# Three blocks of queries turned by VectorE, from 128-byte rows loaded through ScalarE's queue

## The chip, the cores and the metric

The kernel runs on one core of a Trainium2 chip. The metric is the device time in microseconds (us) of one execution. Executions of a kernel differ by some tenths of a per cent: the three of the kernel before took 1526.53, 1528.02 and 1528.81 us.

## What is computed

A linear attention, an RMS norm, and two feed-forward layers, all in float32 (batch 8, heads 8, sequence 576, head width 64; 4608 tokens of width 512; hidden width 2048):

```python
kv  = einsum('bhsd,bhse->bhde', k, v)
out = einsum('bhsd,bhde->bhse', q, kv)
x   = out / sqrt(mean(out * out, -1) + 1e-6) * g_norm     # heads side by side: 4608 x 512
h   = x @ w_in;   x = (max(h, 0) + alpha * min(h, 0)) @ w_out
h   = x @ w_in2;  x = (h / (1 + exp(-1.702 * h))) @ w_out2
```

## The kernel before

**Tiling.** The 4608 tokens are nine blocks of 512 (j = 0 to 8). Each float32 matrix is split into a high and a low part that TensorE multiplies as float32r, so a product is three matmuls of 128x512 (`mm3`, L1078). Blocks 1 to 8 go through the layers in pairs with a scheme that needs seven products instead of eight (`pair_in`, `pair_out`); block 0, half of the hidden width of block 1, and of block 2, go through plainly (`plain`, `gemm_in`, `gemm_out`).

**Stages.** First comes block 0's attention. Then `plain` walks the list `segs` of the first layer: block 0's hidden chunks 0 to MH-1, block 1's chunks 0 to 7, block 0's chunks MH to 15, block 2's chunks 0 to 7, two sets of six or twelve matmuls per chunk and direction. After that `pairs` runs the pairs of both layers. The weights are converted as the kernel runs (`weight`, `sums`: ScalarE, VectorE, GpSimd) and written to DRAM, from where SyncE's queue (SP) loads them back piece by piece (L1266).

**Attention of the later blocks.** For block j, `job_q_later` has SP load the queries of its 512 tokens, all heads, in 256-byte rows (one row is one head of one token; L639), 128 tokens in each of four DMAs, one more where a block lies across two batches. For each pair of heads p, TensorE turns the four 128x128 pieces into one PSUM bank (L655), and ScalarE copies the bank to the tile `qT` (L663). `job_out` multiplies `qT` with the batch's key-value product (L684), ScalarE copies the result out (L729), and the norm follows. `job_x` has VectorE turn the normed block in squares of 32x32 (L755). These jobs are dealt among the steps of the main line by the table JOBS (block: first half step, number of half steps); J1 does so for block 1. So blocks 6 to 8 fall into the first half of `pairs`.

**Order.** Every operation is first noted (`note`) with its engine and a cost. A planner in the kernel (`arrange`) then lays all of them out in time, with due times made of the constants (AHEAD, SPARE, SHIFT, the ..._WAY triples, RINGS and others) and a list OPENING for the first microseconds, and gives out buffers; each engine then executes its instructions in the order so found. That order is fixed when the kernel is built: on the chip, an engine whose next instruction waits doesn't take a later one.

**A bank's turn in `pairs`.** Steps with two hidden chunks alternate, and each step is six matmuls in, six out. A first-layer bank (X, Z) is written by six matmuls, copied out by ScalarE (L1362) or added by VectorE (L1354), and written again after three other groups of six.

Of the kernel before, what the change touches and what calls it, by code (L numbers as in the profile page):

```python
# [10 lines left out]
F32 = mybir.dt.float32  # L11
# [8 lines left out]
P = 128  # L20
# [1 line left out]

LAG = 2

MH = 6
EARLY = ()


# [1 line left out]
SEQ = "q0 q1 o0 q2 q3 x0 x1 o1 x2 x3"  # L30

K1 = (0, 1)
J1 = (1, 6)


PLAIN = 3
HALF = 4
KEPT = 4
MID = 0
SUM_SLACK = -20.0  # L40
XD = 2

JOBS = {2: (12, 12), 3: (32, 12), 4: (43, 12), 5: (63, 23), 6: (100, 16), 7: (124, 22), 8: (153, 16)}


P_IN = (1, 2, 6, 5, 3, 7, 4)
# [7 lines left out]

MM, TR, ACT, DVE, POOL, ISSUE, LAND, RATE, HOP = 0.227, 0.109, 0.63, 0.67, 1.27, 0.55, 2.2, 0.335, 0.2
ACT2, DVE2, POOL2 = 1.06, 1.17, 2.8
KB1, B128, B256, B512 = 1.1, 2.9, 1.77, 1.3

HOP_ASIDE = 0.8
AHEAD = {'wt': 9.6, 'xs': 30.3, 'xc': 40.9, 'gr': 7.1, 'ld': 13.7, 'raw': 50.7, 'w2p': 46.7, 'x': 14.7}  # L60
SLACK = 10.0
SPARE = {'8': 1, '4': 3, '2': 2}
SPARE_W = {'8': 1, '4': 2, '2': 7}

BACKLOG = 2.0
URGENT = 10.0
LD_LOW = {'4': 15}
ADDS = 4
PASSES = 1
AHEAD_START = {'wt': 22.5, 'xs': 24.0, 'xc': 74.6, 'gr': 8.0, 'ld': 16.2, 'raw': 299.2, 'w2p': 67.1, 'x': 12.0}  # L70
AHEAD_LATER = {'wt': 5.4, 'xs': 64.6, 'xc': 171.8, 'gr': 8.1, 'ld': 7.1, 'raw': 192.8, 'w2p': 20.7, 'x': 11.7}
SPARE_LATER = {'8': 3, '4': 6, '2': 6}
SPARE_W_LATER = {'8': 4, '4': 1, '2': 1}
LD_LOW_LATER = {'4': 15}
EARLY_T = 420.0
LEAD = 25.0
START_T = 60.0
AFTER = {}
OPENING = {
# [14 lines left out]
}  # L94
FILLED = 42.0
WAKE, SPARE_TIME = 2.5, 0.7
LATE = 0
START_WAY = (0.74, 28.59, 3.37)
FIRST_WAY = (1.12, 18.86, 1.66)
LATER_WAY = (1.14, 8.81, 1.95)  # L100
SHIFT = {
# [20 lines left out]
}  # L122
SEED = 14
GAP, SLOW = 1.8, 3.4

RINGS = (3, 1, 2, 9)

UNITS = 110
UNIT = 512
# [8 lines left out]
def linear_attention_two_ffn_kernel(  # L138
# [120 lines left out]
    def spare_of(now, later):  # L259
        return now if pe_clock[0] < EARLY_T else later  # L260
# [20 lines left out]
    def tl(key):  # L281
        return tiles[key]

    def arrange(before, first, later, shift, stop=None):
# [6 lines left out]
        for o in ops:  # L291

            if o.eng == "PE":
                o.early = o.clock < EARLY_T
                o.late = before[o.n] if before and not o.early else o.clock + LEAD
                now_ = o.late + o.cost
                o.base = o.late
            else:
                o.late = now_ + o.slack if o.slack is not None else 1e9
                o.early = now_ < EARLY_T + LEAD  # L300
            o.land = o.cost + (LAND + o.mb / RATE if o.eng == "SP" else 0.0)
        for o in reversed(ops):
            o.way = START_WAY if o.early and o.clock < START_T else first if o.early else later
            late = [a.late - o.way[2] * (HOP if a.eng != o.eng else 0.0) - o.land for a in after[o.n]]
# [127 lines left out]
        for _ in range(len(ops)):  # L432
# [33 lines left out]
            start[o.n] = t  # L466
            free_at[o.eng] = t + cost
            fin[o.n] = t + cost
            if o.eng == "SP":
                dma_at = max(dma_at, t + cost) + o.mb / RATE  # L470
                fin[o.n] = dma_at + LAND
            changed = {o.eng}
# [54 lines left out]
    def runs(t0, n):  # L527
        done = 0
        while done < n:
            b, s = divmod(t0 + done, S)  # L530
            step = min(n - done, S - s)
            yield done, step, b, s
            done += step
# [66 lines left out]
    def job_q(j, p):  # L600

        if j:
            return job_q_later(j, p)
        bank, qT, src = ("qTps", j, p), ("qT", j, p), ("ldq", j, p)

        def load():
            for h in range(2):
                nc.sync.dma_start(
                    out=tl(src)[:, h * TB // 2 : (h + 1) * TB // 2],
                    in_=q[0, 2 * p + h, 0:TB, :].rearrange("(p t) d -> p (t d)", t=NT4),  # L610
                )

        def fn():
            for t in range(NT4):
                to = tl(bank)[:, t * P : (t + 1) * P]
                nc.tensor.transpose(to[0:D], tl(src)[:, t * D : (t + 1) * D], ident)
                nc.tensor.matmul(to[D:P], lhsT=tl(src)[:, (NT4 + t) * D : (NT4 + t + 1) * D], rhs=ident, start=True, stop=True)

        note(
            "SP", 2 * ISSUE, load, writes=[(src, 0)], new=[(src, [P, TB], F32, "2")],  # L620
            ahead=ahead_of("ld"), slack=None, mb=0.26 * KB1,
        )
        held_by[qT] = turn_of("qT", RINGS[3])
        note(
            "PE", 12 * TR, fn, reads=[(src, 0)], writes=[(bank, 0), held_by[qT]],
            new=[(bank, [P, TB], F32, "a")], aside=True, idle=lambda: tl(bank)[:, 0:P],
        )
        note(
            "ACT", ACT, lambda: nc.scalar.copy(tl(qT), tl(bank)), reads=[(bank, 0)], writes=[(qT, 0)],
            new=[(qT, [P, TB], F32, "2")], low={"2": 3},  # L630
        )

    def job_q_later(j, p):
# [30 lines left out]
            new=[(qT, [P, TB], F32, "2")], low={"2": 3},  # L664
        )

    def q_of(j, p):

        return ("qT", j, p), lambda: tl(("qT", j, p))

    def job_out(j, pp):

# [920 lines left out]
```

## Time and profile before

| | |
|---|---|
| median of three executions | 1528.02 us |
| profiled execution: its time, its span | 1526.27 us, 1524.5 us |
| TensorE busy | 1508.5 us (99%) |
| VectorE busy | 1165.7 us (76%) |
| ScalarE busy | 784.8 us (51%) |
| GpSimd busy | 338.3 us (22%) |
| queue of SP: share of the 16 DMA engines' span | 81.2% |

The span goes from the first to the last instruction; the time has 1.8 us more around it. An engine's busy time doesn't hold its waits, nor the instructions that issue a DMA, so an engine can be shown idle while it issues. Matmuls overlap (each is shown for some 390 ns and the next begins sooner), so what a matmul costs is read from start to start.

### The profile page before, as it was taken

The numbers are of one execution on the slowest core, as the hardware profiler recorded it, in microseconds if no ns is written. First come the engines' busy times: TensorE is split into PE (matmuls) and PEld (weight loads), VectorE is DVE, ScalarE is ACT, GpSimd is POOL, SyncE is SP. The second block draws the span as 40 slices with busy tenths as digits, with TensorE's granted clock in tenths as the row PEclk, the third lists the DMA queues.
The fourth block names the chain that finished last, engine by engine and source line by source line (L and its number), as shares of the span: only waits on it lengthen the run. The fifth ranks groups of instructions, "written<-read, shape, count | busy, mean of one in ns | idle before, by whom it ended". The sixth has DMA issues, their size and how long they took to land.

```text
span 1524.5 us, 19956 instructions
## 1 busy us (share of the span) xinstructions
PE 1508.5 (99%) x7430; PEld 1244.7 (82%) x7430; DVE 1165.7 (76%) x1175; ACT 784.8 (51%) x985; POOL 338.3 (22%) x298
## 2 busy tenths in 40 slices
PE   8999999999999999999999999999999999999999
PEld 6787878788888888888888888888888888888887
DVE  5999997988789999998999776556665665557511
ACT  5875764545554655545556555445544554445222
POOL 3487727402100335133416210000000000000000
PEclk9999999999999999999999999999999999999999
DMA  9996898989987899979999976687668666766970
GB/s 285 298 324 204 245 365 282 322 279 334 334 309 240 266 347 332 342 277 359 341 318 335 358 265 221 207 247 237 194 206 252 232 193 207 237 193 206 314 253 34
DMA packets 243329, 411.34 MB, mean 270 GB/s; under 512 B 90528, under 2 KB 122528, under 8 KB 243232
## 3 DMA queue, kind: packets, MB, share of 16 engines
q1 hardware_dynamic: 243232, 410.06, 81.2%
q8 instruction: 59, 0.97, 0.3%
q14 instruction: 38, 0.31, 0.1%
HBM read 318.78 MB, written 91.23 MB: 269 GB/s over the span
## 4 chain that ended last, share of the span: by engine, by line
PE 79%; DVE 11%; issue 2%; ACT 1%; POOL 0%; DMA 0%; SPq 0%; DVEq 0%; ACTq 0%
PE V L1078 19%; PE X L1078 19%; PE W L1078 15%; PE Z L1078 14%; PE y L1078 5%; PE h L1078 4%; DVE gr L832 1%; PE ops L684 1%; DVE xc L832 1%; DVE da L904 1%; DVE gl L1042 1%; DVE gt L1301 1%; DVE x L832 1%; DVE w L832 1%; DVE g L1042 1%
## 5 line engine op out<-in xcount | busy, mean ns | idle before, releaser
L1078 PE MATMUL X<-xc,pi 128*128 128x512 f32 x1332 | 338.8, 390 | 0.8 <-DVE xc L832 0.5
L1078 PEld LDWEIGHTS X<-xc,pi 128*128 128x128 f32 x1332 | 249.4, 188 | 53.2 <-DVE xc L832 0.9
L1078 PE MATMUL Z<-xc,pi 128*128 128x512 f32 x984 | 249.7, 389 | 0.2
L1078 PEld LDWEIGHTS Z<-xc,pi 128*128 128x128 f32 x984 | 184.4, 188 | 39.4 <-DVE gt L1354 1.2
L1078 PE MATMUL V<-gr,po 128*128 128x512 f32 x852 | 216.4, 389 | 0.0
L1078 PEld LDWEIGHTS V<-gr,po 128*128 128x128 f32 x852 | 159.8, 188 | 33.3 <-issue 0.2
L1078 PE MATMUL W<-gr,po 128*128 128x512 f32 x624 | 157.7, 389 | 0.0
L1078 PEld LDWEIGHTS W<-gr,po 128*128 128x128 f32 x624 | 117.1, 188 | 24.4
L825 ACT ACTIVATE gr<-gt 128x1024 fp32r<-128x1024 f32 x90 | 95.0, 1060 | 77.8 <-PE W L1078 26.2
L1078 PE MATMUL V<-gr,pi 128*128 128x512 f32 x492 | 124.4, 389 | 0.0
L832 DVE TENSOR_TENSOR gr<-gt,gr 128x1024 fp32r<-128x1024 f32 x90 | 110.9, 1237 | 9.0 <-ACT gr L825 9.0
L832 DVE TENSOR_TENSOR gr<-gl,gr 128x1024 fp32r<-128x1024 f32 x60 | 78.1, 1303 | 45.8 <-ACT gr L825 45.7
L1078 PEld LDWEIGHTS V<-gr,pi 128*128 128x128 f32 x492 | 92.2, 188 | 19.0
L1078 PE MATMUL h<-x,w 128*128 128x512 f32 x390 | 100.6, 398 | 2.4 <-DVE x L790 2.1
L1078 PE MATMUL W<-gr,pi 128*128 128x512 f32 x408 | 102.9, 389 | 0.0
L1078 PEld LDWEIGHTS W<-gr,pi 128*128 128x128 f32 x408 | 76.6, 188 | 15.9
L1078 PEld LDWEIGHTS h<-x,w 128*128 128x128 f32 x390 | 73.4, 191 | 18.3 <-DVE x L790 2.7
L825 ACT ACTIVATE gr<-gl 128x1024 fp32r<-128x1024 f32 x60 | 63.6, 1061 | 43.5 <-PE V L1078 25.8
L1362 ACT ACTIVATE gt<-X 128x512 f32<-128x512 f32 x64 | 38.2, 597 | 70.3 <-PE X L1078 68.9
L1352 DVE TENSOR_TENSOR gt<-Z,gt 128x512 f32<-128x512 f32 x64 | 43.9, 687 | 38.1 <-PE Z L1078 37.6
L1003 POOL TENSOR_TENSOR da<-da 128x256 f32<-128x256 f32 x52 | 61.1, 1176 | 46.6 <-DVE wsp L832 32.3
L1372 ACT ACTIVATE gt<-gt 128x1024 f32<-128x1024 f32 x32 | 33.8, 1060 | 55.3 <-DVE gt L1352 55.3
(487 smaller groups left out, 2555.7 us busy)
## 6 DMA issues: line engine op xcount, KB each, us to landing
pi<-w1wi SPq DMA_DIRECT2D x115, 512.0 KB, 4.6
pi<-w0wi SPq DMA_DIRECT2D x81, 512.0 KB, 5.9
po<-w1wo SPq DMA_DIRECT2D x73, 512.0 KB, 3.6
po<-w0wo SPq DMA_DIRECT2D x52, 512.0 KB, 5.4
pi<-w1wo SPq DMA_DIRECT2D x41, 512.0 KB, 3.7
pi<-w0wo SPq DMA_DIRECT2D x35, 512.0 KB, 5.8
raw<-in_moe_w_in_dram SPq DMA_DIRECT2D x16, 1024.0 KB, 8.0
raw<-in_moe_w_out_dram SPq DMA_DIRECT2D x16, 1024.0 KB, 7.6
```

What stands on the lines that cost most here:

```text
L684: nc.tensor.matmul((tl(("ops", j, heads[i])) if j else tl(bank)[:, i])[off : off + n, t], lhsT=q_of(j, heads[i])[1]()[:, t * P + off : t * ...
L825: "ACT", ACT2 if both else ACT, lambda: nc.scalar.activation(out=part(0), in_=value(), func=AF.Copy, scale=1.0 if scale is None else scale),
L832: nc.vector.tensor_tensor(out=part(1), in0=value(), in1=high, op=ALU.subtract)
L904: nc.vector.scalar_tensor_tensor(out=x, in0=y, scalar=0xC0000000, in1=x, op0=ALU.bitwise_and, op1=ALU.bitwise_or)
L1003: lambda o=o, a=a, b=b, op=op: nc.gpsimd.tensor_tensor(out=quarter(o), in0=quarter(a), in1=quarter(b), op=op),
L1042: nc.vector.scalar_tensor_tensor(out=o, in0=o, scalar=alpha_sb[:, m : m + 1], in1=o, op0=ALU.mult, op1=ALU.max)
L1078: nc.tensor.matmul(o, lhsT=x, rhs=y, start=start and n == 0, stop=stop and n == 2, skip_group_check=True)
L1301: "DVE", DVE2, lambda: nc.vector.tensor_tensor(out=o[0](), in0=a[0](), in1=b[0](), op=ALU.subtract),
L1352: nc.vector.tensor_tensor(out=val(), in0=tl(bank), in1=val(), op=ALU.add)
L1362: nc.scalar.activation(out=val(), in_=tl(bank), func=func, scale=sign)
L1372: lambda: nc.scalar.activation(out=tl(g)[:, :, kk], in_=tl(g)[:, :, kk], func=AF.Gelu_apprx_sigmoid),
```

## The change

Queries of blocks 6 to 8 (j >= TURN = 6) take another way. `job_q_turned` loads two pairs of heads (half a block) at a time so that a 32-float row (128 bytes, half of one head of one token) lands where squares of 32x32, turned in place by one VectorE instruction, give `qT` for both pairs. TensorE's sixteen turns a block, and ScalarE's four copies, are gone there. The loads are issued by ScalarE (`nc.scalar.dma_start`), two DMAs in one noted operation; a block has 32, 32 and 16 of them (blocks 6, 7, 8), for which the planner counts 0.5 us each. `q_of` hands out halves of the wider tile.

The planner now counts landing time for any operation that loads, not SP's alone. MH goes from 6 to 10 and block 1's jobs move later by J1; the table JOBS, the constants, the number of buffers (RINGS), OPENING and SHIFT are all different, so the order of work is another one throughout. The number of multiplying matmuls is the same.

```diff
-MH = 6
+MH = 10
-J1 = (1, 6)
+J1 = (4, 10)
+TURN = 6
-SUM_SLACK = -20.0
+SUM_SLACK = -40.0
-JOBS = {2: (12, 12), 3: (32, 12), 4: (43, 12), 5: (63, 23), 6: (100, 16), 7: (124, 22), 8: (153, 16)}
+JOBS = {2: (13, 14), 3: (33, 16), 4: (48, 13), 5: (64, 23), 6: (89, 29), 7: (119, 23), 8: (152, 28)}
-KB1, B128, B256, B512 = 1.1, 2.9, 1.77, 1.3
+KB1, B128, B256, B512 = 1.1, 2.2, 1.77, 1.3
-LATE = 0
+LATE = 2
-RINGS = (3, 1, 2, 9)
+RINGS = (2, 2, 3, 6)
...
-            o.land = o.cost + (LAND + o.mb / RATE if o.eng == "SP" else 0.0)
+            o.land = o.cost + (LAND + o.mb / RATE if o.mb else 0.0)
...
-            return job_q_later(j, p)
+            return job_q_later(j, p) if j < TURN else job_q_turned(j, p // 2) if p % 2 == 0 else None
...
+    def job_q_turned(j, pp):
+        src, qT = ("ldq", j, pp), ("qT", j, pp)
+        todo = []
+        for off, n, b, s in runs(TB * j, TB):
+            u = off // 32
+            if n // 32 < 4:
+                todo += [(u + x, None, b, s + 32 * x, n) for x in range(n // 32)]
+            else:
+                todo += [(u, p, b, s, n) for p in range(2)]
+        def load(i, u, p, b, s, n):
+            h, a = i // 2, i % 2 * 32
+            to = tl(src)[32 * i : 32 * (i + 1)].rearrange("x (p n f) -> x p n f", p=2, f=32)
+            if p is None:
+                nc.scalar.dma_start(
+                    out=to[:, :, u],
+                    in_=q[b, 4 * pp : 4 * pp + 4, s : s + 32, a : a + 32].rearrange("(p h) x f -> h x p f", h=2)[h],
+                )
+            else:
+                nc.scalar.dma_start(
+                    out=to[:, p, u : u + n // 32],
+                    in_=q[b, 4 * pp + 2 * p + h, s : s + n, a : a + 32].rearrange("(n x) f -> x n f", x=32),
+                )
+        pieces = [(i, *x) for i in range(4) for x in todo]
+        for n in range(0, len(pieces), 2):
+            note(
+                "ACT", 2 * 0.5, lambda n=n: [load(*x) for x in pieces[n : n + 2]], reads=[(src, 0)] if n else [],
+                writes=[(src, n)], new=[] if n else [(src, [P, 2 * TB], F32, "4")], ahead=ahead_of("ld"), slack=None,
+                mb=0.52 * B128 / len(pieces), low=spare_of(LD_LOW, LD_LOW_LATER) if j > 1 else None,
+            )
+        held_by[qT] = turn_of("qT", RINGS[3])
+        note(
+            "DVE", DVE2, lambda: nc.vector.transpose(tl(qT), tl(src)),
+            reads=[(src, n) for n in range(0, len(pieces), 2)], writes=[(qT, 0), held_by[qT]],
+            new=[(qT, [P, 2 * TB], F32, "4")], low={"4": 2},
+        )
```

## Rows read from the trace of the kernel before

**Rows 1.** Page, part 1: busy time, share of the span and instructions.

```profile
span 1524.5 us, 19956 instructions
PE 1508.5 (99%) x7430; PEld 1244.7 (82%) x7430; DVE 1165.7 (76%) x1175; ACT 784.8 (51%) x985; POOL 338.3 (22%) x298
```

**Rows 2.** Windows: busy time (instructions) of each engine, clock, DMA share, GB/s.

```profile
25.00:50.00 25.00, 22.52 (x183) 18.64 (x182) 22.67 (x33) 17.75 (x22) 12.11 (x13) 0.93 1.05 301
50.00:75.00 25.00, 24.13 (x139) 19.15 (x137) 22.47 (x30) 20.84 (x34) 13.42 (x13) 1.00 1.03 305
...
300.00:525.00 225.00, 224.47 (x1198) 185.68 (x1197) 200.30 (x210) 119.44 (x148) 34.65 (x28) 1.00 0.89 296
525.00:850.00 325.00, 324.30 (x1435) 267.38 (x1434) 314.51 (x295) 179.62 (x205) 119.05 (x95) 1.00 0.93 332
```

**Rows 3.** PE's waits, five of the list of 13: us in total, times, longest.

```profile
PE y L1078 <- DVE x L832: 3.7, 2, 2.1
PE h L1078 <- DVE x L790: 2.1, 2, 1.8
PE kvps L514 <- POOL ident masks.py:199: 1.4, 1, 1.4
...
PE kvps L567 <- DMA kR<-in_v_dram: 0.7, 1, 0.7
...
PE qTps L655 <- ACT qT L663: 0.2, 1, 0.2
```

**Rows 4.** Timeline of PE, block 8's turns: start, us, instruction, count [idle before].

```profile
504.79 1.52 PE L1078 MATMUL X<-xc,pi 128*128 128x512 f32 x6
506.15 1.52 PE L1078 MATMUL W<-gr,po 128*128 128x512 f32 x6
...
512.96 0.60 PE L655 MATMUL qTps<-ident,ldq 128*128 128x128 f32 x4
513.31 1.64 PE L1078 MATMUL X<-xc,pi 128*128 128x512 f32 x6
514.79 0.61 PE L655 MATMUL qTps<-ident,ldq 128*128 128x128 f32 x4
...
518.85 0.60 PE L655 MATMUL qTps<-ident,ldq 128*128 128x128 f32 x4
519.75 1.63 PE L1078 MATMUL X<-xc,pi 128*128 128x512 f32 x6 [0.29 <-ACT xs L729]
```

**Rows 5.** The same for two of block 6's turns.

```profile
347.66 1.04 PE L655 MATMUL qTps<-ident,ldq 128*128 128x128 f32 x8
348.93 2.05 PE L684 MATMUL ops<-kvb,xs 128*128 128x128 f32 x16 [0.24 <-ACT xs L663]
```

**Rows 6.** Instructions of L655 in the whole span: ns min/median/max, first and last start.

```profile
L655 PE MATMUL qTps<-ident,ldq x128: 270/272/329, 52.9 to 519.2; 128*128 128x128 f32 x128
```

**Rows 7.** One ScalarE copy of a turned bank, one VectorE turn of 14, one eviction group.

```profile
L663 ACT COPY da<-qTps x9: 567/586/592, 53.5 to 520.7; 128x512 f32<-128x512 f32 x9
...
L755 DVE STREAM_TRANSPOSE t<-g x1: 1245/1245/1245, 484.3 to 484.3; 128x1024 f32<-128x1024 f32 x1
...
L1362 ACT ACTIVATE gt<-X,sign_sb 128x512 f32<-128x512 f32 x56 | 38.0, 684 | 42.8 <-PE X L1078 35.9 <-PE W L1078 4.2 <-PE V L1078 2.1
```

**Rows 8.** SP's DMA issues by line (ns min/median/max), and L639's time to landing.

```profile
L639 SPq DMA_DIRECT2D ldq<-in_q_dram x36: 383/728/6890, 17.4 to 465.0; - x36
DMA to landing us min/median/max: 3.6/5.4/14.1
...
L1452 SPq DMA_DIRECT2D out_dram<-acc x16: 337/509/1793, 982.8 to 1431.4; - x16
...
L1266 SPq DMA_DIRECT2D pi<-w1wi x112: 319/319/1271, 777.4 to 1382.0; - x112
```

**Rows 9.** Timeline of SP while block 8's queries are loaded.

```profile
457.59 0.38 SPq L639 DMA_DIRECT2D ldq<-in_q_dram  x1
...
463.40 5.39 SPq L639 DMA_DIRECT2D ldq<-in_q_dram  x3
468.89 0.80 SPq L1266 DMA_DIRECT2D pi<-w0wo  x1
```

**Rows 10.** Page, part 3: queues with packets, MB, share of 16 engines.

```profile
q1 hardware_dynamic: 243232, 410.06, 81.2%
q8 instruction: 59, 0.97, 0.3%
```

More of the change, by code (lines that the diff above doesn't have):

```diff
@@ L56 @@
 ACT2, DVE2, POOL2 = 1.06, 1.17, 2.8
-KB1, B128, B256, B512 = 1.1, 2.9, 1.77, 1.3
+KB1, B128, B256, B512 = 1.1, 2.2, 1.77, 1.3
 HOP_ASIDE = 0.8
-AHEAD = {'wt': 9.6, 'xs': 30.3, 'xc': 40.9, 'gr': 7.1, 'ld': 13.7, 'raw': 50.7, 'w2p': 46.7, 'x': 14.7}
+AHEAD = {'wt': 6.7, 'xs': 25.0, 'xc': 59.6, 'gr': 6.8, 'ld': 33.5, 'raw': 34.3, 'w2p': 426.3, 'x': 15.2}
 SLACK = 10.0
-SPARE = {'8': 1, '4': 3, '2': 2}
-SPARE_W = {'8': 1, '4': 2, '2': 7}
-BACKLOG = 2.0
+SPARE = {'8': 5, '4': 8, '2': 7}
+SPARE_W = {'8': 1, '4': 1, '2': 4}
+BACKLOG = 1.1
 URGENT = 10.0
-LD_LOW = {'4': 15}
+LD_LOW = {'4': 13}
 ADDS = 4
 PASSES = 1
[L70 to L75, printed above, removed]
+AHEAD_START = {'wt': 188.2, 'xs': 92.0, 'xc': 152.4, 'gr': 92.0, 'ld': 11.6, 'raw': 574.8, 'w2p': 119.4, 'x': 63.4}
+AHEAD_LATER = {'wt': 14.8, 'xs': 44.1, 'xc': 614.6, 'gr': 7.9, 'ld': 10.3, 'raw': 229.7, 'w2p': 73.1, 'x': 657.3}
+SPARE_LATER = {'8': 4, '4': 3, '2': 7}
+SPARE_W_LATER = {'8': 3, '4': 6, '2': 2}
+LD_LOW_LATER = {'4': 8}
+EARLY_T = 410.0
 LEAD = 25.0
@@ L79 @@
 OPENING = {
[1 row of a table removed]
[1 row of a table added]
     ('SP', ('ldkv', 0, 1), 0): -97.0, ('SP', ('ldq', 0, 1), 0): -96.0, ('SP', ('raw', 0, 'wi', 0), 0): -95.0,
[2 rows of a table removed]
[2 rows of a table added]
     ('SP', ('raw', 0, 'wo', 0), 0): -88.0, ('SP', ('alpha',), 0): -87.0, ('ACT', ('qT', 0, 0), 0): -50.0,
[9 rows of a table removed]
[7 rows of a table added]
+    ('ACT', ('dr_', 0, 'wi', 0), 0): -36.0,
 }
@@ L96 @@
 WAKE, SPARE_TIME = 2.5, 0.7
-LATE = 0
-START_WAY = (0.74, 28.59, 3.37)
-FIRST_WAY = (1.12, 18.86, 1.66)
-LATER_WAY = (1.14, 8.81, 1.95)
+LATE = 2
+START_WAY = (1.33, 16.72, 2.5)
+FIRST_WAY = (0.93, 11.18, 3.32)
+LATER_WAY = (0.61, 27.37, 0.69)
 SHIFT = {
[20 rows of a table removed]
[22 rows of a table added]
 }
@@ L468, in arrange @@
             fin[o.n] = t + cost
-            if o.eng == "SP":
+            if o.mb or o.eng == "SP":
                 dma_at = max(dma_at, t + cost) + o.mb / RATE
@@ L665, in job_q_later @@
         )
+    def job_q_turned(j, pp):
[33 more added lines that the diff above has]
+        )
     def q_of(j, p):
-        return ("qT", j, p), lambda: tl(("qT", j, p))
+        turned = j >= TURN
+        key = ("qT", j, p // 2 if turned else p)
+        return key, lambda: tl(key)[:, p % 2 * TB : (p % 2 + 1) * TB] if turned else tl(key)
     def job_out(j, pp):
```

64 rows, old and new, of tables (OPENING, SHIFT) are left out of this document.

## Prediction

> **What bounds the kernel now.** I read the page's busy times first: TensorE is busy for 1508.5 of 1524.5 us, VectorE for 1165.7, ScalarE for 784.8 [rows 1]. So TensorE is the bound, and an edit pays by what it takes off TensorE's queue or off TensorE's waits. Next I read the waits of TensorE: thirteen kinds, 11.6 us in all, the largest 3.7 and 2.1 us, both on VectorE, and a single one on a load, of 0.7 us [rows 3]. Then the windows: in the stretch where blocks 6 to 8 are prepared (300 to 525 us) TensorE is busy for 224.5 of 225 us at full clock, VectorE for 200.3, ScalarE for 119.4, and the DMA engines for 0.89 of the time; from 525 to 850 us VectorE is busy for 314.5 of 325 us [rows 2]. VectorE is thus the second engine and close behind, up to 850 us. Last I read the timeline around the turns of block 8, to see what one turn costs on TensorE from start to start [rows 4].
>
> **What goes from TensorE.** Six multiplying matmuls take 506.15 - 504.79 = 1.36 us from start to start. A group of four turns takes 513.31 - 512.96 = 0.35 us, and the six matmuls behind it take 514.79 - 513.31 = 1.48 us, 0.12 us more than six elsewhere [rows 4]. So a group of four between matmuls costs 0.47 us, not the 4 x 272 ns that its shown durations add to [rows 6], which overlap. A block has four such groups and three blocks change: 12 x 0.47 = 5.6 us. The bounds: where a group stands next to other small matmuls, the 0.12 us stays for those, and 12 x 0.35 = 4.2 us goes; where a group's wait goes with it, two of 0.29 and 0.24 us are in the rows [rows 4, 5], 5.6 + 0.5 = 6.1 us goes. I take 5.6, since most groups stand between matmuls.
>
> **What goes from ScalarE and SP.** Twelve copies of 0.586 us, 7.0 us [rows 7], and on SP the 13 loads of these blocks (4, 5 and 4). SP is held for up to 6.9 us in one such issue, and for 5.39 us in three of block 8, with a weight load queued behind them [rows 8, 9]. TensorE waits for no weight load [rows 3], so this is worth nothing by itself; it lets weight loads behind them go earlier.
>
> **What comes to VectorE.** Six turns of 128x1024, in shape those of L755, at 1.245 us [rows 7]: 7.5 us. VectorE has 225 - 200.3 = 24.7 us free in 300 to 525 us, and 10.5 us in 525 to 850 us [rows 2]. I cost the turns at nothing, hidden by that idle time. Were there no room, the conversions of the second layer's weights that follow would end up to 7.5 us later, and TensorE would wait for part of it where the second layer's pairs begin.
>
> **What comes to ScalarE.** 32 + 32 + 16 = 80 DMA issues. None is issued from ScalarE before, so I bound one by SP's: 0.319 us for a weight load in whole rows, 0.337/0.509/1.793 us (least, median, most) for stores of 512 rows of 256 bytes, 0.728 us in the median for the query loads of 1024 rows [rows 8]. The new ones have at most 512 rows, so I take 0.51 us: 41 us, between 80 x 0.319 = 26 and 80 x 0.728 = 58 us. Of 225 us, ScalarE would then have 119.4 - 7.0 + 41 = 153 busy or issuing, 170 at the upper bound. It has room on average. What counts is how long it is held at a stretch. A bank of the pairs is closed, must be copied out in 0.684 us [rows 7], and is written again after three groups of six, 3 x 1.36 = 4.1 us [rows 4]. So ScalarE may come 3.4 us late before TensorE waits. Two issues as one operation, 1.0 us by the median, fit three times over. Behind them in ScalarE's queue stand those copies and the splitting of `gr` and `xc`; TensorE waits for the copies first.
>
> The Trainium skill, page "Perfetto Trace Analysis", section "DMA Instruction — HWDGE (DVE, Sync)", says that the shown span of such an issue holds the wait for a descriptor generator that the issuing engines share, and the generating itself. It would have ScalarE stand behind SP's long issues too; no run here shows it yet, since SP issues alone.
>
> **What comes to the DMA engines.** The same bytes in rows half as long, 12,288 more rows. Bounds: nothing more, if a row's time goes by bytes; or twice the time per block, if it goes by rows. Three loads of 0.79 MB were issued in 5.39 us [rows 9], so a block of 1.05 MB takes about 7.2 us, and twice that adds 3 x 7.2 = 22 us to a stretch with 225 x 0.11 = 25 us free [rows 2]. A store of 512 short rows is issued in 0.337 us at least and a load of whole rows in 0.319 us [rows 8], so the count of rows weighs little there, and I take a third of the upper end, 7 us, spread over the stretch and hidden by the loads' lead.
>
> The Trainium skill speaks against the short rows: "DMA: Bandwidth & Descriptors", section "Specifications", wants 512 bytes or more for full rate. The rows here, with 256 bytes, land in 5.4 us in the median, which by itself shows no such loss; by the page the sum would keep its 5.6 us and only the lead needed would grow.
>
> **The new order.** MH, J1, LATE, OPENING, RINGS and all due times change. The number of multiplying matmuls doesn't. The first stretch of block 0 now needs the fifth pair of weight chunks by its ninth step, where before it was not needed until after block 1's half; block 1's inputs come due four steps later. VectorE is busy for 22.7 and 22.5 of 25 us there [rows 2]. What this can give is at most the waits that end in VectorE's work, of which 3.7 + 2.1 us are the largest [rows 3]; what it can take isn't bounded by a row, and I let it be as much. I take zero, between -5.8 and +5.8 us: one plan with few waits takes the place of another.
>
> **Sum.** Against the profiled execution: 1526.27 - 5.6 = 1520.7 us (its span 1524.5 and 1.8 around it). That execution lies 1.75 us below the median of the runs, 1528.02, so the forecast for the median is 1528.02 - 5.6 = 1522.4 us.
>
> **Rivals.**
>
> *ScalarE or VectorE stands behind the loads (slower).* All queues are in order. If an issue from ScalarE is held as SP's were, 5.39 us at a stretch [rows 9], the bank copies come 5.39 - 3.4 = 2.0 us too late, once for each of the six half-block loads: 12 us, 1522.4 + 12 = 1534.4 us. With the longest single issue, 6.89 us [rows 8], it is 6 x 3.5 = 21 us, 1543 us. The same holds for VectorE if its turn waits for rows that land late: it also empties banks, by the same cover. It decides from 3.4 us of hold; with an average hold of 3.4 + 5.6 / 6 = 4.3 us the change is worth nothing. For it: DMA engines at 0.89, and landing times of up to 14.1 us [rows 8]. Against it: the new issues are half as long or shorter, two at a time, and most of SP's are under 1 us.
>
> *The gain is given back (within 0.2%).* VectorE's 7.5 us find no room where they stand, or the new order waits half as much again as the 11.6 us of now [rows 3]: 5.6 us of waits come for 5.6 us of turns, 1528.0 us. For it: VectorE at 314.5 / 325 = 0.97 from 525 us on. Against it: the 24.7 us free before that [rows 2].
>
> *The start gains as well (faster).* The new opening and the later block 1 take away some two thirds of the 3.7 + 2.1 us that TensorE waits for VectorE [rows 3]: 4 us more, 1518.4 us.
>
> That the change doesn't do what it says can't well be: the matmuls of L655 are either issued for three blocks or not.
>
> **How the numbers follow.** Forecast 1522.4 us: 0.46. The start gains as well, 1518.4 us: 0.10. Given back, 1528.0 us: 0.20. Held queues, 1534.4 us and above: 0.24. Faster by over 0.2% (3.1 us, about what a measurement can tell from no change) is then 0.56, the same 0.20, slower 0.24. The range goes from 1517, a little under the best case, to 1536, over the first size of the slower one; its larger size, and a plan that fails at the start, lie beyond, with no more than 2 in 10.
>
> **What the profile after would show.** 80 rows of turns of L655 for blocks 1 to 5 instead of 128; six VectorE turns more and twelve ScalarE copies fewer; a second queue of some 3 MB beside SP's, which now carries 410.06 MB [rows 10]; TensorE busy for about 1503 us. Right: in 300 to 525 us TensorE's idle time is still near 0.5 us, and issues on ScalarE are near 0.5 us each. Wrong: single issues of over 3 us on ScalarE with waits of X, Z or their copies behind them; a VectorE turn that waits for its load; or waits of over 12 us in the first 300 us, which would lay it on the order and not on the turns.

## The result and the profile after

The changed kernel takes 1539.14 us in the median of four executions (1538.59 to 1542.86); the kernel before, run beside it, 1528.41 us (1526.53 to 1530.78, four). The ratio is 1.0075, 95% interval 1.0053 to 1.0096: slower by 0.75%, 10.7 us. The forecast was 1522.4 us, faster, with a range up to 1536; the time lies outside it, on the side of the rival of the held queues. The profiled execution took 1539.61 us.

Two parts of the page of the changed kernel: busy times, and the queues (packets, MB, share of 16 engines). They answer to [rows 1, 10].

```profile
span 1537.8 us, 19978 instructions
...
PE 1513.4 (98%) x7401; PEld 1246.9 (81%) x7401; DVE 1166.3 (76%) x1181; ACT 769.9 (50%) x973; POOL 332.4 (22%) x298
...
q1 hardware_dynamic: 230736, 406.91, 79.9%
q10 hardware_dynamic: 25856, 3.15, 1.4%
```

The second queue is there with its 3.15 MB. TensorE is busy for longer than before, 1513.4 against 1508.5 us, though 48 turns are gone: some of its work ran at half clock, where the same work is shown as more busy time, and at the start 19 more small matmuls fill gaps.

The windows (TensorE, weight loads, VectorE, ScalarE, GpSimd busy; granted clock; DMA share; GB/s), against [rows 2]:

```profile
25.00:50.00 25.00, 21.46 (x152) 18.33 (x151) 23.89 (x31) 17.64 (x25) 12.38 (x12) 0.93 1.05 310
50.00:75.00 25.00, 25.00 (x199) 20.40 (x198) 24.25 (x29) 21.72 (x31) 13.27 (x12) 1.00 0.86 258
300.00:525.00 225.00, 217.54 (x1118) 178.98 (x1117) 203.31 (x211) 108.63 (x130) 34.23 (x28) 0.98 0.89 289
525.00:850.00 325.00, 323.78 (x1442) 267.58 (x1441) 294.77 (x286) 171.36 (x197) 90.49 (x75) 1.00 0.89 308
340.00:425.00 85.00, 78.59 (x414) 64.80 (x412) 71.16 (x77) 32.20 (x39) 18.85 (x16) 0.96 0.89 269
```

Where the queries of blocks 6 to 8 are prepared, TensorE's idle time went from 0.5 us to 225 - 217.5 = 7.5 us; 6.4 of it lie in 340 to 425 us, and the clock there is 0.96. VectorE is hardly busier there than before (203.3 against 200.3 us), and ScalarE is busy for less (108.6 against 119.4). TensorE's waits in the whole span (us in total, times, longest), against [rows 3]:

```profile
PE ops L727 <- ACT gl L1405: 6.4, 3, 3.1
PE h L1121 <- DVE x L833: 1.8, 1, 1.8
...
PE Z L1121 <- DMA gs<-w0wi: 1.2, 1, 1.2
```

The largest is new and is behind a ScalarE eviction, L1405 (L1362 before), of `gl`. Here is the stretch that ends in one of these waits, as ScalarE and its queue (ACTq) went through it (start, us, engine, instruction, count, and in brackets the idle time before it with its end):

```profile
346.94 7.28 ACTq L689 DMA_DIRECT2D da<-in_q_dram  x8
354.32 1.06 ACT L868 ACTIVATE gr<-gt 128x1024 fp32r<-128x1024 f32 x1 [6.32 <-DMA da<-in_q_dram]
354.35 3.07 ACTq L689 DMA_DIRECT2D da<-in_q_dram  x4
357.46 0.69 ACT L1405 ACTIVATE gl<-X,sign_sb 128x512 f32<-128x512 f32 x1 [2.08 <-issue]
```

and TensorE:

```profile
353.54 1.52 PE L1121 MATMUL V<-gr,pi 128*128 128x512 f32 x6
358.20 1.16 PE L727 MATMUL ops<-kvb,oc 128*128 128x128 f32 x8 [3.15 <-ACT gl L1405]
```

Eight issues take 7.28 us. Yet one issue is short, as the instructions of L689 show (ns least/median/most, first and last start; then who waited for it, in us and times; then the time to landing):

```profile
L689 ACTq DMA_DIRECT2D da<-in_q_dram x16: 317/442/902, 340.7 to 356.5; - x16
...
L689 ACTq DMA_DIRECT2D ldq<-in_q_dram x8: 318/334/1441, 532.4 to 544.9; - x8
...
  ACT gr L868: 24.5, 3
...
DMA to landing us min/median/max: 1.9/4.7/8.9
```

So the time goes between issues, while ScalarE's queue waits. The semaphore numbers in the records of the trace say for what. SP's and ScalarE's DMAs signal their landing on the same eight numbers, in turn, in the order of the program. Before an issue may take a number again, its queue waits for the landing of the DMA that had it last. In the kernel before SP alone used the eight. The issue at 353.42 us is released at 353.40 by the landing of a weight load that SP had issued only at 348.29 us; that load took 5.1 us to land. Counted over the 80 issues, 16 stand behind such a landing for more than 0.1 us, 27 us in all, the longest 6.0 us; each of the 16 starts 0.02 us after the landing (worked out from the records). `gr`'s split, the copy of a bank and in the end TensorE stand behind them.

After such a stall the clock falls. Two windows of the same stretch:

```profile
355.00:360.00 5.00, 1.49 (x10) 1.24 (x10) 4.24 (x5) 2.92 (x5) 2.54 (x2) 0.97 0.96 267
360.00:365.00 5.00, 5.00 (x20) 4.38 (x21) 3.35 (x3) 2.49 (x4) 2.45 (x3) 0.69 0.98 255
```

TensorE is idle for 3.5 of five us, and from 359.7 us on the granted clock is 0.5 for 3.4 us, the level of 1.2 GHz in place of 2.4. The stall of 2.9 us at 397.5 us is followed by the same. By this each stall of some 3 us costs an estimated 1.7 us more, half of the 3.4.

**Two losses in time order.** The multiplying matmul that comes 900th starts at 291.47 us before and at 299.11 us after, with 19 more small matmuls ahead of it, the fillers of the start: 7.6 us are lost by then, ahead of any of the new loads. From there to the end 5.7 us more are lost on balance (span 1524.5 to 1537.8), though the turns give some back. The experiments take the two apart.

### The profile page after: what moved, and what is told of

The parts are those of the page before. It is cut to its first block, busy times and chain, and to the rows that moved or that the text cites. A ratio compares the mean times of both kernels' runs of the same rounds, so it can differ in the third digit from the quotient of the medians.

```text
span 1537.8 us, 19978 instructions
## 1 busy us (share of the span) xinstructions
PE 1513.4 (98%) x7401; PEld 1246.9 (81%) x7401; DVE 1166.3 (76%) x1181; ACT 769.9 (50%) x973; POOL 332.4 (22%) x298
## 3 DMA queue, kind: packets, MB, share of 16 engines
q10 hardware_dynamic: 25856, 3.15, 1.4%
## 4 chain that ended last, share of the span: by engine, by line
PE 84%; DVE 7%; DMA 5%; POOL 2%; ACT 1%; issue 1%; SPq 0%; ACTq 0%; DVEq 0%; POOLq 0%
PE V L1121 19%; PE X L1121 19%; PE W L1121 14%; PE Z L1121 14%; PE h L1121 6%; PE y L1121 6%; PE ops L727 2%; POOL da L955 1%; DVE gr L875 1%; DMA raw<-in_moe_w_in_dram 1%; PE kvps L569 1%; DMA ldq<-in_q_dram 1%; DMA gs<-w0wi 1%; DMA pi<-w0wo 1%; DMA raw<-in_moe_w_out_dram 0%
## 5 line engine op out<-in xcount | busy, mean ns | idle before, releaser
L1121 PE MATMUL V<-gr,pi 128*128 128x512 f32 x1056 | 268.1, 390 | 0.0
L1121 PEld LDWEIGHTS V<-gr,pi 128*128 128x128 f32 x1056 | 197.7, 188 | 41.9 <-issue 0.9
L1121 PE MATMUL X<-xc,pi 128*128 128x512 f32 x816 | 208.7, 392 | 1.3 <-DVE gl L1397 1.3
L1121 PEld LDWEIGHTS X<-xc,pi 128*128 128x128 f32 x816 | 154.0, 189 | 34.1 <-DVE gl L1397 2.2
L1121 PE MATMUL W<-gr,pi 128*128 128x512 f32 x588 | 148.5, 389 | 0.0
L1121 PE MATMUL X<-xc,po 128*128 128x512 f32 x516 | 131.0, 389 | 0.0
L1121 PE MATMUL W<-gr,po 128*128 128x512 f32 x456 | 115.0, 389 | 0.0
L1121 PEld LDWEIGHTS X<-xc,po 128*128 128x128 f32 x516 | 96.8, 188 | 20.0
L1405 ACT ACTIVATE gt<-X 128x512 f32<-128x512 f32 x64 | 38.3, 598 | 137.5 <-PE X L1121 135.9
L1395 DVE TENSOR_TENSOR gt<-Z,gt 128x512 f32<-128x512 f32 x64 | 43.9, 687 | 61.7 <-PE Z L1121 61.6
L1121 PE MATMUL V<-gr,po 128*128 128x512 f32 x300 | 76.1, 390 | 1.1 <-DVE gr L875 0.8
L1121 PEld LDWEIGHTS V<-gr,po 128*128 128x128 f32 x300 | 56.2, 188 | 13.3 <-DVE gr L875 1.1
```

The costliest lines, as they stand in the source:

```text
L1121: nc.tensor.matmul(o, lhsT=x, rhs=y, start=start and n == 0, stop=stop and n == 2, skip_group_check=True)
L1395: nc.vector.tensor_tensor(out=val(), in0=tl(bank), in1=val(), op=ALU.add)
L1405: nc.scalar.activation(out=val(), in_=tl(bank), func=func, scale=sign)
```

## The experiments

Times are medians. Each difference is against runs of the kernel before beside it (1528.41 us for the change, 1529.01 for the next three kernels of the table, 1529.70 for the four behind them, 1529.04 for the last four). Idle is TensorE's idle time in 340 to 425 us of the profiled execution.

| kernel | time, us | against before, us | idle, us |
|---|---|---|---|
| the change | 1539.14 | +10.7 | 6.4 |
| its order, loads issued by SP | 1533.32 | +4.3 | 3.5 |
| the change, fillers in shorter gaps | 1538.02 | +9.0 | 6.2 |
| the change, twice the issues | 1595.04 | +66.0 | 24.6 |
| its order, no turned queries | 1536.69 | +7.0 | 1.4 |
| the change, opening of before | 1547.10 | +17.4 | 11.0 |
| its order, loads issued by GpSimd | 1591.27 | +61.6 | 19.1 |
| loads on SP, planned there | 1536.41 | +6.7 | 4.2 |
| start of before, loads on SP | 1522.47 | -6.6 | 1.7 |
| start of before, loads on ScalarE | 1539.82 | +10.8 | 10.3 |
| start of before, blocks 7 and 8 only, on SP | 1521.64 | -7.4 | 0.2 |
| start of before, no turned queries | 1527.64 | -1.4 | 0.2 |

### Which queue issues the loads

**The same order, issued by SP.**

```diff
-                nc.scalar.dma_start(
+                nc.sync.dma_start(
```

(in both loads; nothing else, so the plan still counts them on ScalarE)

> The changed kernel with its plan untouched, except that the 80 short-row loads are issued from SP's queue at the same places of the program instead of ScalarE's. Theory H (ScalarE is held): ScalarE's issues wait until an earlier DMA has landed, the bank copies behind them come late, and TensorE, which waited 3.1 and 2.9 us at 354.7 and 397.5 us and had its clock at half for 3.4 us after each, pays some 7 to 11 us between 300 and 420 us. Then these waits go, and the time falls from 1539.1 to about 1528 to 1532 us. Rival D (short rows are slow to land, or the DMA engines are full, whoever issues): the turns still come late, 1537 us or more. Rival P (the new plan has these waits in itself): no change, 1539 us.

1533.32 us, +4.3 (ratio 1.0031, 1.0019 to 1.0043). Against the +10.7 of the changed kernel, 6.4 us are gone with one word, a little less than theory H expected (1528 to 1532 us). TensorE's largest wait in 340 to 425 us, and the window:

```profile
PE ops L727 <- ACT gl L1405: 2.3, 1, 2.3
```
```profile
340.00:425.00 85.00, 81.50 (x433) 67.04 (x433) 75.76 (x81) 38.18 (x46) 17.97 (x16) 0.98 0.94 282
```

The idle time falls from 6.4 to 3.5 us. The rows are the same 128 bytes and land no sooner (median 5.0 us against 4.7), so neither the rows nor VectorE's turns make this part of the loss. Not all of it goes: at the same place TensorE still waits 2.3 us behind `gl`, with no load on ScalarE. Here the copy stands behind a split of `gr`, and this behind VectorE, whose turn at 337.5 us had waited for its load and which then has no pause up to 358 us:

```profile
337.50 1.25 DVE L703 STREAM_TRANSPOSE oc<-kvb 128x1024 f32<-128x1024 f32 x1 [2.08 <-DMA kvb<-in_q_dram]
```
```profile
355.57 1.06 ACT L868 ACTIVATE gr<-gl 128x1024 fp32r<-128x1024 f32 x1 [1.90 <-DVE gr L875]
356.54 0.67 ACT L1405 ACTIVATE gl<-X,sign_sb 128x512 f32<-128x512 f32 x1
```

Whether that one late turn makes the wait was not tried.

**Twice the issues, the same rows.** Each load of a whole column is cut in two halves of 16 partitions.

```diff
+                for y in range(0, 32, 16):
...
-                    out=to[:, p, u : u + n // 32],
+                        out=to[y : y + 16, p, u : u + n // 32],
...
```

> The changed kernel with its plan untouched, except that each of the short-row loads in whole columns is cut in two DMAs of 16 partitions: twice the issues, the same rows and bytes. Theory H (what holds ScalarE is the number of DMAs, each waiting for the landing of an earlier one): more and longer holds between 300 and 420 us, 1545 to 1552 us. Rival D (the short rows and the bytes): the same rows, 1538 to 1541 us.

1595.04 us, +66.0 (ratio 1.044, 1.0416 to 1.0464): the way that theory H expected, and far more of it. TensorE's waits in the whole span, and the window:

```profile
PE ops L728 <- ACT gl L1406: 25.5, 2, 14.4
PE V L1122 <- ACT gr L869: 14.6, 3, 8.3
```
```profile
340.00:425.00 85.00, 60.44 (x249) 48.73 (x247) 54.88 (x56) 26.75 (x32) 14.76 (x12) 0.84 0.70 211
```

One issue still takes 0.44 us in the median, so 64 more are 28 us of ScalarE's time, but 55 us more are lost than in the changed kernel; 46 issues are now held, 62 us in all. The loss follows the number of DMAs on ScalarE and the landings that they wait for. The DMA engines are less busy than before (0.70), so they aren't short.

**The same order, issued by GpSimd.** (`nc.gpsimd.dma_start` in both loads.)

> The same plan and the same short rows, but both loads are issued by POOL (GpSimd) instead of ScalarE. Theory H (ScalarE is held because each of its issues waits for the landing of an earlier DMA, and the bank copies stand behind it): ScalarE has no issue and no hold, gl comes in time, TensorE's waits behind gl fall from 6.4 to under 1 us, and the time falls by 6 to 10 us, to 1529 to 1533 us. Theory D (the short rows themselves load the DMA engines so that other loads come late): the rows are the same, so the time stays within 2 us of 1539. Rival Q (POOL's issuing is slow, or POOL's own splits of 1.2 us stand behind the held issues): waits move to tiles that POOL writes (da, oc, kvb) or to VectorE's turns behind their loads, and the time is 1535 us or more.

1591.27 us, +61.6 (ratio 1.0403, 1.0388 to 1.0419). ScalarE is free, but it helped nothing. From the instructions of L689, what its engine stood idle for, and who waited for it (us, times):

```profile
L689 POOL DMA_DIRECT2D oc<-in_q_dram x16: 632/642/652, 398.6 to 450.6; - x16
...
  issue: 78.9, 33
...
  DVE kvb L703: 26.1, 2
  DVE oc L703: 11.1, 1
```

GpSimd's DMAs signal on eight other numbers (111 to 118), and it too pauses between issues, 79 us in 33 pauses by this view, and issues in 0.64 us. But it doesn't pause for a number to come free: wherever a number is used again, the DMA that had it last had landed at least 4.1 us before the issue. Of the 47 pauses of over 0.1 us, 33 end 0.31 us after the landing of the third load before, and ten, all in block 8 with 512 rows in each load, 0.30 to 0.35 us after that of the load just before (worked out from the records). So GpSimd is held as well, by few loads under way at a time, which is another hold than ScalarE's. Now its own conversions and VectorE's turns stand behind, as rival Q has it. This run can't tell short rows from the hold, as it was meant to; the two before it do.

### What the new order costs by itself

**The new order without the turned queries.**

```diff
-TURN = 6
+TURN = 9
```

> The new order without the change of the turns: blocks 6 to 8 are loaded by SP in 256-byte rows and turned by TensorE again; the new constants stay. Theory S (two losses: the new opening and order cost about 7 us by 300 us of the span, the ScalarE loads about 10 us in 340 to 425 us, and the turns give 5.6 us back): the loss of the loads goes and the turns come back, 1539.1 - 10 + 5.6 = 1534.7 us, with no wait of TensorE of over 2 us behind gl in 340 to 425 us and no half-clock stretch there. If the loss lies in the loads alone, this kernel is the kernel before under other constants: 1528.5 us within 1.5. If the order as a whole is bad, also behind the start, 1538 us or more.

1536.69 us, +7.0 (ratio 1.0050, 1.0033 to 1.0066; 5.0 to 10.1 us). No query is turned by VectorE here, no load is on ScalarE, TensorE's idle time in 340 to 425 us is 1.4 us, and still most of the loss is there, between the first and the third case of the expectation. So the order costs 7.0 us, and the turns and their loads, added to it, 3.7 us more; the two intervals overlap, so that the 3.7 may be less or nothing.

Where the order loses is seen at the start. The first multiplying matmuls, of this run and of the changed kernel:

```profile
27.82 2.31 PE L1121 MATMUL h<-x,w 128*128 128x512 f32 x9
```
```profile
31.42 2.31 PE L1121 MATMUL h<-x,w 128*128 128x512 f32 x9
```

Before, the first comes at 25.57 us. In seven profiles with the new opening, it comes at 27.7 to 29.6 us in four and at 31.4 to 32.8 us in three (the changed kernel is one); in the six with the old opening always at 25.5 to 26.0 us. The three late ones run slowly near the start: a turn of L618 takes 0.42 us at 12 us of the span, and 0.30 us in the other four. In the changed kernel the granted clock shows it; the records of the clock in the two others begin only at 19.7 us:

```profile
8.00:18.00 10.00, 9.43 (x68) 6.91 (x65) 1.19 (x2) 4.08 (x8) 0.00 (x0) 0.50 0.96 302
```

So the opening loses 2 to 4 us by its order, and some 4 us more in the three executions in which TensorE runs slowly there. With that goes the 900th matmul: it is 7.6 us late in the changed kernel and 4.5 us late (296.01) here.

**Fillers from the first microsecond.** Small matmuls that keep TensorE at work while it waits are put into shorter gaps.

```diff
-WAKE, SPARE_TIME = 2.5, 0.7
+WAKE, SPARE_TIME = 2.5, 0.0
```

> The changed kernel with its plan untouched, except that TensorE's idle time in the first 42 us is filled more tightly with turns of the identity (the spare 0.7 us of each gap is set to 0). Theory C (start by the clock): the first multiplying matmul begins at 31.4 us instead of 25.6 us because TensorE's clock was at half from 8.1 us for 10.2 us, behind two waits for the query loads at 4.8 and 5.5 us; with the first gap filled the clock stays at full and 4 to 5 us go: 1534 to 1535 us. Rival: the clock falls all the same, or the start is late by its loads and not by the clock: 1538 to 1540 us, first multiplying matmul near 31 us.

1538.02 us, +9.0 (ratio 1.0064, 1.0049 to 1.0079). In its profile no stretch before 43 us is at half clock, and the first matmul comes at 29.63 us; but the time is only 1.7 us nearer to the kernel before, less than the two intervals can tell apart. The half clock at the start is at most the smaller part.

**The old opening alone.** The table OPENING of the kernel before, planned anew.

> The changed kernel with only the table OPENING of the kernel before (the order of the first operations), planned anew; the loads stay on ScalarE. If the opening's order makes the loss at the start, the first multiplying matmul comes back from 31.4 to about 26 us and the time falls by some 5 us to 1534 us; the stalls behind gl in 340 to 425 us stay. If the loss at the start lies elsewhere (due times, depth of buffers), the first matmul comes earlier but the 900th is still some 7 us later than before, and the time stays at 1537 to 1540 us, or goes above where the rest of the new due times doesn't fit the old opening.

1547.10 us, +17.4 (ratio 1.0112, 1.0095 to 1.0129). The first matmul is back at 25.82 us, but the 900th comes at 299.65 us, as late as ever, and TensorE waits 4.0 us behind VectorE and 3.5 us for a weight load further on. The expectation's second case holds: this table put back by itself loses more, so the loss isn't this table's alone. Which of MH, J1 and the due times loses how much behind the start was not tried one by one and stays open.

**Loads on SP, and the order planned for that.** As in the first experiment, with the operation noted on SP.

> The loads on SP as in e1_sp, and the order planned with them there, so that SP's weight loads are put where the loads leave room. Theory H: as in e1_sp ScalarE is free, and what was left of 4.3 us over the kernel before is the start's 5 to 7 us, less the turns' 5.6 us, plus weight loads that stand behind; with the last put elsewhere 1530 to 1532 us. If the planned place of the loads weighs nothing, 1533.3 us as in e1_sp within 1. If SP can't carry 80 issues more, over 1536 us with TensorE's waits on DMAs of the first layer's weights.

1536.41 us, +6.7 (ratio 1.0048, 1.0031 to 1.0065): no better than the order that wasn't planned for SP (+4.3; the intervals overlap). TensorE's waits in 340 to 525 us are now on weight loads:

```profile
PE V L1121 <- DMA po<-w0wo: 3.0, 1, 3.0
PE V L1121 <- DMA pi<-w0wo: 2.9, 2, 1.9
```

The third case of the expectation, though in its profile TensorE also runs slowly near the start (first multiplying matmul at 32.8 us). The planner doesn't know of the eight semaphores; whether that is why its place for the loads is no better was not tried.

### The old start, the turns, and new due times

For these, MH, J1, LATE, RINGS, START_WAY and OPENING are those of the kernel before. The due times behind the start were sought anew.

```diff
-MH = 10
+MH = 6
-J1 = (4, 10)
+J1 = (1, 6)
-LATE = 2
+LATE = 0
-RINGS = (2, 2, 3, 6)
+RINGS = (3, 1, 2, 9)
...
-                nc.scalar.dma_start(
+                nc.sync.dma_start(
```

> The turns of blocks 6 to 8 on VectorE as in the change, but the loads are issued by SP, and the start (MH, J1, the opening, the start's depths) is that of the kernel before; the due times behind it are set anew for this. Theory S + H (the change lost some 7 us by its new order and some 8 us by holding ScalarE, and the turns are worth 5.6 us): both losses go, the first multiplying matmul is near 25.6 us, TensorE idles for under 2 us in 340 to 425 us, and the time is 1522 to 1527 us, below the kernel before. If SP's 80 issues delay weight loads in any order, as in e7_spplan (4 us idle in 340 to 425 us, 4.5 us in 425 to 525 us), 1530 us or more.

1522.47 us, -6.6 (ratio 0.9951, 0.9936 to 0.9966): faster than both kernels. First matmul at 25.75 us, the 900th at 290.47. Of TensorE's waits in 340 to 425 us none is on ScalarE:

```profile
PE Z L1101 <- DMA po<-w0wi: 0.9, 1, 0.9
PE X L1101 <- DMA po<-w0wi: 0.6, 1, 0.6
```

**The same with ScalarE as the issuer**, one word in each load.

```diff
-                nc.sync.dma_start(
+                nc.scalar.dma_start(
```

> f1_sp6 with one edit: its two loads are issued by ScalarE, at the same places of the program. It is the pair of the changed kernel and e1_sp in another order. Theory H (ScalarE is held while its issues wait for landings of earlier DMAs): TensorE waits behind gl or another of ScalarE's evictions in 340 to 525 us, and the time is 4 to 15 us above f1_sp6. If what ScalarE lost in the changed kernel belonged to that one order, the two agree within 2 us.

1539.82 us, +10.8 (ratio 1.0066, 1.0051 to 1.0082). One word costs 17.4 us, more than the 4 to 15 expected. 17 of the 80 issues are held here for the landing that had their number last, 23 us in all (worked out from the records). TensorE's waits in the same stretch:

```profile
PE Z L1101 <- DVE gt L1377: 4.8, 1, 4.8
PE V L1101 <- DMA po<-w0wo: 1.4, 1, 1.4
PE Z L1101 <- ACT gl L1385: 1.3, 1, 1.3
```

How the largest of them comes about, from the last load of a half block to TensorE:

```profile
350.86 0.35 ACTq L669 DMA_DIRECT2D xn<-in_q_dram  x1
357.96 1.25 DVE L683 STREAM_TRANSPOSE qT<-xn 128x1024 f32<-128x1024 f32 x1 [3.56 <-PE V L1101]
361.67 0.75 DVE L1377 SCALAR_TENSOR_TENSOR gt<-Z,sign_sb,gt 128x512 f32<-128x512 f32 x1
362.48 2.93 PE L1101 MATMUL Z<-xc,po 128*128 128x512 f32 x6 [4.75 <-DVE gt L1377]
```

The issue at 350.86 us was held for 1.9 us by the landing of a weight load of SP, and its own load landed at 357.78 us. VectorE's turn stood for 3.6 us, until then (the view names TensorE, which was done 0.04 us sooner), and behind the turn stood the emptying of a bank. With SP as the issuer the same turn starts at 351.3 us. So here the late load reaches TensorE by way of VectorE. The longest hold of ScalarE comes right behind:

```profile
362.72 10.74 ACTq L669 DMA_DIRECT2D ldkv<-in_q_dram  x9
373.51 0.69 ACT L1385 ACTIVATE gt<-X,sign_sb 128x512 f32<-128x512 f32 x1 [10.12 <-DMA po<-w0wo]
```

Nine issues hold ScalarE for 10.7 us, where issues take 0.32 to 0.49 us in the median; yet TensorE has no wait from 362.5 to 380 us. A hold costs only what stands behind it in time. The pair is the clearest of the runs: same opening, same rows, same turns, same plan. That plan counts the loads on SP, so part of the 17.4 us may be that it doesn't suit ScalarE; this order planned for ScalarE was not tried.

**Blocks 7 and 8 only** (`TURN = 7`, loads on SP, due times of its own).

> As f1_sp6, but only blocks 7 and 8 are turned on VectorE (48 issues of short rows instead of 80, 8 groups of turns gone from TensorE instead of 12, 3.7 us), with due times of their own. Theory S + H: 1523 to 1528 us. If each block's loads on SP cost more than the 1.9 us that its turns are worth, this one is faster than f1_sp6 by some us.

1521.64 us, -7.4 (ratio 0.9944, 0.9927 to 0.9961). Not to be told from three blocks. Whether the third block's 1.9 us of turns go into its 32 loads on SP, or into due times that differ, these runs don't separate.

**New due times alone**: the kernel before, its start kept, its turns on TensorE.

> The kernel before with nothing of the turns changed, and due times set anew in the same way as in f1_sp6 and f2_sp7; start and opening stay. It tells what the new due times alone are worth. If f1_sp6's gain is that of the turns, this one stays within 3 us of the kernel before, 1526 to 1530 us; if the gain is that of the due times, it is as fast as f1_sp6.

1527.64 us, -1.4 (ratio 0.9987, 0.9978 to 0.9997). So the faster kernel's gain isn't that of a new search for due times: against this one the turns give 1527.64 - 1522.47 = 5.2 us. Each of the two has due times of its own, so this is no measure of the turns to the tenth: two blocks give 6.0 us in the same way, where 3.7 were expected.

## Why the prediction was wrong

Put together: the order costs 7.0 us; the turns give 5.6 us back (forecast; 5.2 measured in the pair of the last section); what is left of +10.7 is 10.7 - 7.0 + 5.6 = 9.3 us for the new loads. Of these, 6.4 us went away with the issuer: ScalarE's hold, with the half clock behind its stalls. The other 2.9 us stay with SP as the issuer, and their cause stays open. The order's cost has an interval of some 2.5 us to either side and the change's of some 3, so the 9.3 has some 4; in the other order one word took away 17.4 us.

**What goes from TensorE: right.** Forecast 5.6 us, between 4.2 and 6.1; the pair gives 5.2, as far as kernels with different due times can tell.

**What goes from ScalarE and SP: right as far as it went**, with no worth by itself. It missed that SP's issues and the new ones stay tied by the semaphores.

**What comes to VectorE: right.** Six turns of 1.24 us; VectorE has 21.7 us free in 300 to 525 us. One turn waits for its load (1.6 us), and a bank's copy waits for that turn, as one of the signs of being wrong had it.

**What comes to ScalarE: the step that failed.** One issue was taken at 0.51 us and is 0.44 us; 80 are 35 us, below the 41. The sum was sized well and counted the wrong thing. "How long it is held at a stretch" was the right question, but the answer given, two issues of 1.0 us against a cover of 3.4 us, took the issue for the hold. The hold that came is the wait ahead of an issue: 27 us in 16 issues, and 7.3 us over eight issues in a row. It ends with another DMA's landing, 5.1 us for the weight load at 348.29 us, so the length of the new issues has nothing to do with it.

The 5.39 us for three issues in [rows 9], from which the rival was priced, were something else: the last of the three took 3.78 us by itself, and the DMA that had its number last had landed 4.9 us before (worked out from the records). Against holds of that kind the prediction's argument, that the new issues are "half as long or shorter", was right: of the 80, one is over 1.2 us. It didn't ask what an issue waits for before it begins.

The Trainium skill, "DMA: Bandwidth & Descriptors", section "Issuing engines are not separate DMA queues", says that DMAs begun on several engines share the 16 DMA engines, and that another issuer saves only the time of issuing. The runs agree on the landing (medians 4.7 us from ScalarE, 5.0 us from SP) and show besides that the change of issuer can cost 17.4 us. The other page of the Trainium skill that the prediction weighed, "Perfetto Trace Analysis", section "DMA Instruction — HWDGE (DVE, Sync)", with its shared descriptor generator, isn't borne out as a price here: the median issue of 0.44 us is that of the same issues on SP (0.43 us). One issue agrees with it: the longest, of 1.44 us, runs beside an issue of 2.04 us on SP and ends with it, at 534.2 us.

**What comes to the DMA engines: right in kind.** The 3.15 MB take 1.4% of 16 engines over 1537.8 us, 21.5 us; at the mean rate of SP's queue before (410.06 MB in 81.2% of 1524.5 us) they would take 9.5 us. So 12 us more, within 0 to 22, above the 7 taken. The share in 300 to 525 us is 0.89 both times, and none of TensorE's waits there is on a load.

**The new order: the second step that failed.** Taken at zero within 5.8 us; it costs 7.0, with an interval from 5.0 to 10.1. The bound took the plan's waits for all that an order can lose. Fillers, half clock and a later first matmul don't show among those waits: in the first 300 us TensorE is idle for 11.8 us after and 10.9 before, while 7.6 us are lost.

**The rivals.** The rival of the held queues came true in what it said of the outcome, ScalarE's copies too late and TensorE waiting for them, but not in its mechanism. Its price, 12 us from a hold of 5.39 us at each of six half-block loads, is near the 9.3 us by luck: the waits behind `gl` are three, 6.4 us in all and 3.1 us at most, with the half clock behind two of them. Its chance, 0.24, was too low. It left out the order's loss, which takes the time beyond its 1534.4 us and beyond the range. The other two didn't happen.

**The signs.** "Idle near 0.5 us in 300 to 525" failed with 7.5 us, as it should. "Single issues of over 3 us" would have missed the cause: none is over 1.5 us. "Waits of over 12 us in the first 300 us", the sign for the order, would have missed it too, with 11.8 us idle. The sign is the span of a run of issues in the queue's row (7.28 us for eight).

## What to carry over

Before DMAs are moved to a computing engine, ask what each issue has to wait for, not only how long it takes: here every DMA of the two queues reused one of eight semaphores, so no issue could begin before an earlier DMA had landed, and everything on the engine stood behind that. Such issues did best here on SP, the queue that computes nothing, and the hold shows as the time that a run of issues spans. And where a change comes with a new order of work, price the order by itself: it cost here at least about what the change gave.

## What the runs showed of the hardware

- A stall of TensorE of some 3 us (3.15 us at 355, 2.86 us at 397.5) was followed each time by 3.4 us at a granted clock of 0.5, with TensorE at work.
- With the same opening, TensorE ran slowly near the start in three of seven profiles (a turn of L618 in 0.42 us instead of 0.30; at a granted clock of 0.50 from 8 to 18 us in the changed kernel) and not in the others, and the first multiplying matmul came some 4 us later. Why some executions are so stays open.
- GpSimd's issues of the same loads pause for another reason than ScalarE's: of 47 pauses of over 0.1 us, 33 end 0.31 us after the landing of the third load before and ten, with 512 rows in each load, 0.30 to 0.35 us after that of the load just before, while the number that each uses had been free for 4.1 us or more.
- An issue that waits for a landing is shown no longer for it: the 16 held issues of the changed kernel waited up to 6.0 us and took 0.32 to 0.35 us.
